# A dynamic convolution with a maxout block: one load, two warming products and one exponential moved or left out in the opening

## The chip, the cores and the metric

The kernel runs on one core of one Trainium2 chip, as one program. The metric is the device time of an execution in microseconds. Three executions of the kernel before took 410.79 to 412.25 us, with a median of 411.01 us.

## The reference

Inputs are x (8 sequences of 4160 positions with 192 features), weight_gen (for each position 8 heads with 7 logits) and three matrices: w1 and w2 (192 x 1024) and w_out (1024 x 192). Cut to what is computed:

```python
w = exp(weight_gen - max(weight_gen, -1)); w = w / (sum(w, -1) + 1e-09)
x_pad = concatenate([zeros(B, 6, D), x], axis=1)
out[b, s, h, :] = sum_k w[b, s, h, k] * x_pad[b, s + k, head h]     # 24 features to a head
h1 = out @ w1; h2 = out @ w2
result = maximum(h1, h2) @ w_out                                    # 33280 x 192, float32
```

So each position mixes itself and the six positions before it, with a softmax over the seven taps that differs by position and head, and the mixed rows go through two matrices, a maximum and a third matrix.

## The kernel before

The 33280 rows are laid over 128 partitions of 260 consecutive positions each. A "column" is one position on every partition. Columns are taken in batches of 16 (`BATCHES`); in the first two batches a batch is cut into four units of four columns, later into units of eight. The columns are rotated: what the code calls column 0 is column 8 of x (`actual`), so `load_x(0, 4, 4)`, four columns of batch 0 from its fifth on, loads columns 12 to 15 of x. The tile of x for a batch, `xb_t`, has six columns of halo and then sixteen.

The maximum is rewritten: maximum(h1, h2) @ w_out = h1 @ w_out + relu(h2 - h1) @ w_out. So the kernel forms the difference of w2 and w1 once on VectorE (`w_diff`, into `wd`, from the staged tiles `ws0` and `ws1`, whose parts are named E for the first 128 rows and T for the last 64), and the product of w1 and w_out once on TensorE (`w10_product`).

Work on a batch goes through these steps, and the lines are those that the profile names:

- `load_wg` (L115) loads logits, `load_x` (L133) loads x and converts it to bf16. `exp_sum` (L162, ScalarE) makes the exponentials, `red` (L180, VectorE) sums them over the taps, `ln` (L186, ScalarE) takes the logarithm of the sums, `shift` (L191, VectorE) subtracts it from the logits, and `weights` (L202, ScalarE) makes the softmax weights by a second exponential.
- `mul` (L218) and `mul_pair` (L227), both VectorE, multiply x by the weights for all seven taps into `m_t`. `mul_pair` takes one pair of columns, or some of its taps.
- For the early units TensorE sums the taps and transposes at once: `sum_transpose` and `sum_part` (L307) are products with the identity into `yps`, and ScalarE copies the result to `yt` (L316). Later units are summed on VectorE (`adds`, L244, L250, L253) and transposed by DMA (L262).
- `hid_tile` (L362, TensorE) multiplies `yt` by `wd`, `relu` (L372, ScalarE) moves the result to `rd_t`, and `out_first` and `out_second` (L402, L415, TensorE) form the results, which `evac` (L487, ScalarE) copies to `o_t`. In each group, `hidden` orders these steps; `relay` is an empty step on ScalarE that waits for the last product of `out_first`.

The order of the instructions on each engine is written out by hand in the opening (up to group 8, about 60 us) and follows from a table of due times later. Every engine takes its instructions in the order in which the program emits them. Loads of x go out on POOL's queue; the loads of the opening's logits and weights go out on SP's. `behind(first, load)` makes a load wait on its queue until the instruction `first` is done.

The opening matters here. SP issues the first logits, the first ten columns of x as float32 (`xs`, in three loads, converted on VectorE at L679), the first halves of the weights, the second half of the first logits, the other halves of the weights, and the second logits. VectorE's order is: sum and shift of the first half of the logits; the conversions; `mul_pair(0, 0, 0)`, the first pair's product; `mul_pair(0, 0, 1)`; `w_diff("E", 0, 0)`; `mul_pair(0, 4, 0, 0, 4)`, four taps of the second unit's first pair; `w_diff("T", 0, 2)`; `mul_pair(0, 4, 0, 4, K)`, the other three taps; `mul_pair(0, 4, 1)`; `red(0, 1, 2)`; `w_diff("E", HF, 1)`. The four taps read only columns that `xs` brought; the other three taps and the next pair read columns 12 to 15 of x. TensorE meanwhile runs products that serve no result, on a tile called `warm` (`keep_warm`, L672): 18 at the start, 8 behind the first pair's product, and 2 between the second half of `sum_transpose(0)` and `halves_swapped(2)` (L692). The latter is a product that swaps the partition halves of `wd`, copied by ScalarE at L694.

In the loop over the later groups, group 5 is the one the third edit touches. There `hidden` emits the first relu, the relay, then whatever is handed in as `amid`, the last hidden tile, the last relu, the second part of the results with their copy, and then `between`.

Of the kernel before, what the change touches and what calls it, by code (L numbers as in the profile page):

```python
# [17 lines left out]
def _sub(base: bass.AP, off: int, dims):  # L18
    ap = [list(base.ap[0])] + [[int(s), int(c)] for s, c in dims]
    return dataclasses.replace(base, offset=base.offset + off, ap=ap)  # L20
# [3 lines left out]
def kernel(  # L24
# [30 lines left out]
    def pieces(b):  # L55
        n = BATCHES[b][1]
        at, done = [], 0
        for w in (4, 4, 4, 4) if b < 2 else (8, 8) if n == 16 else (n,):
            at.append((done, w))
            done += w  # L60
        return at
# [44 lines left out]
    def actual(v):  # L106
        return v + 8 if v < LAST - 8 else v - (LAST - 8) if v < LAST else v
# [14 lines left out]
    def x_at(b, o):  # L122

        c = BATCHES[b][0] + o
        key, at = (b, o) if c < LAST - 8 else ("wrap", 0) if c < LAST else (NB - 2, 8)
        if key not in xb_ts:
            xb_ts[key] = pxb.tile([P, (16 + PAD) * D], BF16, name="xb_t", tag="xb")
        return xb_ts[key], at * D

    def load_x(b, o, n, halo=True):  # L130

        t, at = x_at(b, o)
        load = nc.gpsimd.dma_start(  # L133
            out=t[:, at + PAD * D:at + (PAD + n) * D],
            in_=bass.AP(tensor=x.tensor, offset=actual(BATCHES[b][0] + o) * D,
                        ap=[[CPP * D, P], [1, n * D]]),
        )
        if 0 < b < NB - 1 and o == 0 and halo:
            load_halo(b)
        if "wrap" in xb_ts and t is xb_ts["wrap"]:  # L140
            nc.gpsimd.memset(t[0:1, 0:PAD * D], 0.0)
            nc.gpsimd.dma_start(
                out=t[1:P, 0:PAD * D],
                in_=bass.AP(tensor=x.tensor, offset=(CPP - PAD) * D, ap=[[CPP * D, P - 1], [1, PAD * D]]),
            )
        return load
# [5 lines left out]
    def load_halo(b):  # L152

        nc.gpsimd.dma_start(out=x_at(b, 0)[0][:, 0:PAD * D],
                            in_=xb_ts[b - 1][:, 16 * D:(16 + PAD) * D])


    def exp_sum(b, i=0, of=1):
        if i == 0:
            e_ts[b] = pe_.tile([P, BATCHES[b][1] * WGC], FP32, name="e_t", tag="e")  # L160
        w = BATCHES[b][1] * WGC // of
        return nc.scalar.activation(out=e_ts[b][:, i * w:(i + 1) * w], in_=wg_ts[b][:, i * w:(i + 1) * w], func=AF.Exp)  # L162

    def part(b, i, of):

        n = BATCHES[b][1]
        h0, h1 = n * i // of * H, n * (i + 1) // of * H
        return slice(h0, h1), h0 * K, [[K, h1 - h0], [1, K]]
# [4 lines left out]
    def sums(b, hs):  # L173

        at = BATCHES[b][0] * H - (0 if b < FIRST else s_parts[0].shape[-1])
        return s_parts[b >= FIRST][:, at + hs.start:at + hs.stop]

    def red(b, i=0, of=1):
        hs, at, ap = part(b, i, of)
        nc.vector.reduce_sum(out=sums(b, hs), in_=_sub(e_ts[b], at, ap), axis=AX.X)  # L180
# [13 lines left out]
    def weights(b, o):  # L194

        w = dict(pieces(b))[o]
        if b not in en_ts:
            en_ts[b] = pen.tile([P, 16 * WGC * 2], BF16, name="en_t", tag="en")
        J = 2 if w == 4 and b < 2 else 1
        N = w * H // J  # L200
        for j in range(J):
            nc.scalar.activation(  # L202
                out=_sub(en_ts[b], (o * WGC + j * N * K) * 2, [[2 * N, K], [2, N], [1, 2]]),
                in_=_sub(wg_ts[b], (o * H + j * N) * K, [[1, K], [K, N], [0, 2]]), func=AF.Exp,
            )
# [77 lines left out]
    LEFT = (0, 1, 2, K - 1)  # L283

    def sum_transpose(u, taps=range(K), amid=lambda: None, now=True):

        copy = sum_part(u, 0, 3, taps)
        amid()
        sum_part(u, 3, 6, taps)
        if now:  # L290
            copy()
        return copy
# [32 lines left out]
    def behind(first, load):  # L325

        tc.add_manual_dep(load.ins, first.ins.name, SYNC, reason="its place among the transfers")
# [288 lines left out]
    with tc.tile_pool(name="pstage", bufs=1) as pstage:  # L616
# [40 lines left out]
        nc.vector.tensor_single_scalar(out=msk_i, in_=msk_i, scalar=RPB - 1, op=ALU.bitwise_and)  # L657
        nc.vector.tensor_single_scalar(out=msk_i, in_=msk_i, scalar=1, op=ALU.min)
        nc.vector.tensor_copy(out=msk, in_=msk_i)
        first_exp = exp_sum(0, 0, 2)  # L660
        for step in (red, ln, shift):
            step(0, 0, 2)
        weights(0, 0)
# [3 lines left out]
        def keep_warm(times, first=False):  # L667

            for _ in range(times):
                nc.tensor.matmul(warm[:, 0:512], lhsT=ident[:, 0:P],  # L672
                                 rhs=_sub(m_t, 0, [[P, 8], [1, 64]]) if first else _sub(ident, 0, [[0, 4], [1, P]]),
                                 start=True, stop=True, skip_group_check=True)

        keep_warm(18)
        for j, parts in enumerate((((0, PAD), (PAD, 2)), ((PAD + 2, 2),))):
            for at, n in parts:
                nc.vector.tensor_copy(out=xb_ts[0][:, at * D:(at + n) * D], in_=xs[:, at * D:(at + n) * D])  # L679
            first_mul = mul_pair(0, 0, j)  # L680
            if j == 0:
                keep_warm(8, True)
        w1 = {kind: pstage.tile([P, w], BF16, name="w1" + kind)
              for kind, w in (("E", F), ("T", HF))}

        def w_diff(kind, c, to):
            nc.vector.tensor_tensor(out=wd[:, to * HF:(to + 1) * HF], in0=ws[kind, 1][:, c:c + HF],
                                    in1=ws[kind, 0][:, c:c + HF], op=ALU.subtract)
# [9 lines left out]
        w1t = pstage.tile([P, F + HF], BF16, name="w1t")  # L698

        w_diff("E", 0, 0)  # L700
        behind(first_exp, load_x(0, 4, 4))
        behind(first_mul, load_x(0, 8, 4))
        load_x(0, 12, 4)
        for h in range(2):
# [8 lines left out]
            nc.sync.dma_start_transpose(out=w1t[:, c0:c0 + w].rearrange("p (b t) -> p b t", t=P), in_=w1[kind])  # L713
        mul_pair(0, 4, 0, 0, 4)
        sum_transpose(0, amid=lambda: halves_swapped(0, warm[:, 512:1024]))
        keep_warm(2)
        w_diff("T", 0, 2)
        halves_swapped(2, warm[:, 0:512])
        mul_pair(0, 4, 0, 4, K)
# [175 lines left out]
    none = lambda: None  # L895
    begun = {}

    def first_of_sum(u):
        begun[u] = sum_part(u, 0, 3)

    def rest_of_sum(u):
        sum_part(u, 3, 6)
        begun[u]()
# [2 lines left out]
        3: (none, rest_of_1),  # L906
        4: (lambda: (behind(relu_of[8], load_x(2, 0, 8, halo=False)),
                     rest_of_sum(4), behind(yt_of[4], load_wg(4, nc.gpsimd)), ln(2)), end_of_1),
        5: (lambda: (exp_sum(3), red(3), sum_transpose(5, LEFT), weights(2, 0)), none),
        6: (lambda: (weights(2, 8), ln(3), rest_of_sum(6)), none),  # L910
        7: (lambda: (behind(relu_of[14], load_x(2, 8, 8)), rest_of_sum(7)), none),
    }
# [76 lines left out]
    for g in range(4, len(GROUPS)):  # L989
        if GROUPS[g][1] == 3 and "c" not in ps:  # L990
            later_ps()
        tiles = [t for t in range(GROUPS[g][0], sum(GROUPS[g])) if t >= 16]
        if g == 9:
            behind(relu_of[16], load_x(3, 0, 8))
        if g in early:
            hidden(g, OUTS[g], early[g][0],
                   amid=lambda: first_of_sum(g) if g != 5 else None)
            early[g][1]()
            steps(g, tiles)
        else:  # L1000
            hidden(g, OUTS[g], beside=lambda: steps(g, tiles))
# [35 lines left out]
```

## Time and profile before

| | |
|---|---|
| median of three executions | 411.01 us (410.79 to 412.25) |
| the profiled execution | 411.17 us |
| its span, first to last instruction | 409.4 us |
| mean granted TensorE clock | 0.997 |
| TensorE busy | 398.0 us |
| VectorE busy | 377.2 us |
| ScalarE busy | 353.8 us |
| data moved by DMA | 66.32 MB, mean 162 GB/s |

A row of a timeline gives the start and the length in us, the engine, the line, the operation, what is written from what, and a count; in brackets the idle time of the engine just before and what ended it. PE is TensorE, PEld its weight loads, DVE VectorE, ACT ScalarE, POOL GpSimd, and SPq or POOLq are the queues' issuing. A row of the chain gives start, length and work of one piece of the chain that ended last; "issue" is time in which the engine waited for nothing that the profile shows. A row of waits gives who waited for whom, with total us, times and the longest. A row of DMA issues gives the median us from issue to landing. Consecutive instructions of an engine overlap a little, so a next one may start somewhat ahead of the end of the one before.

### The profile page before, as it was taken

The numbers are of one execution on the slowest core, as the hardware profiler recorded it, in microseconds if no ns is written. First come the engines' busy times: TensorE is split into PE (matmuls) and PEld (weight loads), VectorE is DVE, ScalarE is ACT, GpSimd is POOL, SyncE is SP. The second block draws the span as 40 slices with busy tenths as digits, with TensorE's granted clock in tenths as the row PEclk, the third lists the DMA queues.
The fourth block names the chain that finished last, engine by engine and source line by source line (L and its number), as shares of the span: only waits on it lengthen the run. The fifth ranks groups of instructions, "written<-read, shape, count | busy, mean of one in ns | idle before, by whom it ended". The sixth has DMA issues, their size and how long they took to land.

```text
span 409.4 us, 16186 instructions
## 1 busy us (share of the span) xinstructions
PE 398.0 (97%) x7406; PEld 317.0 (77%) x7406; DVE 377.2 (92%) x230; ACT 353.8 (86%) x418; POOL 81.2 (20%) x108
## 2 busy tenths in 40 slices
PE   8799999999999999999999999999999999999995
PEld 3588899777777877777777777877787777777795
DVE  6999999999999999999999999999999999999400
ACT  3889899999899998898988999999999889898781
POOL 1411012212221202221221122222111223120000
PEclk9999999999999999999999999999999999999998
DMA  8997298876657665776765676587478558835323
GB/s 242 250 176 208 66 194 152 170 170 164 162 114 210 188 141 117 231 200 87 230 186 109 143 217 188 107 214 187 103 120 250 145 107 228 171 79 158 98 79 120
DMA packets 65110, 66.32 MB, mean 162 GB/s; under 512 B 49425, under 2 KB 54161, under 8 KB 65040
## 3 DMA queue, kind: packets, MB, share of 16 engines
q1 hardware_dynamic: 56064, 40.54, 36.9%
q0 software_dynamic: 8832, 24.63, 29.3%
q8 instruction: 58, 0.95, 0.9%
q10 hardware_dynamic: 144, 0.10, 0.1%
q14 instruction: 12, 0.10, 0.1%
HBM read 37.33 MB, written 25.56 MB: 154 GB/s over the span
## 4 chain that ended last, share of the span: by engine, by line
PE 89%; ACT 6%; DMA 1%; issue 1%; SPq 1%; DVE 0%; ACTq 0%
PE op_ps L402 40%; PE hd L362 38%; PE op_ps L415 7%; ACT rd_t L372 3%; PE hdp L362 2%; PE yps L307 2%; DMA ws1T<-in_moe_w_dram 1%; ACT yt L316 1%; ACT e_t L162 0%; ACT o_t L487 0%; SPq L642 0%; ACT en_t L202 0%; SPq L625 0%; ACT xb_t L150 0%; SPq L634 0%
## 5 line engine op out<-in xcount | busy, mean ns | idle before, releaser
L372 ACT ACTIVATE rd_t<-hd 128x1024 bf16<-128x1024 f32 (+1 forms) x206 | 234.5, 1187 | 26.2 <-PE hd L362 25.0
L402 PE MATMUL op_ps<-wo,rd_t 64*128 64x192 bf16 x4160 | 210.6, 243 | 0.4 <-issue 0.4
L402 PEld LDWEIGHTS <-rd_t 64*128 64x128 bf16 x4160 | 180.8, 94 | 16.0 <-issue 0.6
L362 PE MATMUL hd<-yt,wd 64*128 64x512 bf16 (+1 forms) x1584 | 187.3, 360 | 0.4 <-ACT rd_t L372 0.4
L218 DVE TENSOR_TENSOR m_t<-xb_t,en_t 128x10752 bf16<-128x10752 bf16 (+1 forms) x35 | 181.5, 5191 | 0.8 <-ACT en_t L202 0.5
L362 PEld LDWEIGHTS <-wd 64*128 64x128 bf16 x1776 | 93.9, 94 | 44.8 <-issue 3.6
L270 POOL CAST gate<-yt 128x1 f32<-128x1 bf16 x29 | 42.1, 1451 | 257.8 <-DMA yt<-y_t 257.8
L244 DVE TENSOR_TENSOR m_t<-m_t 128x4608 bf16<-128x4608 bf16 (+1 forms) x30 | 74.1, 2470 | 0.1
L487 ACT COPY o_t<-op_ps 128x384 f32<-128x384 f32 (+1 forms) x99 | 57.1, 587 | 12.4 <-PE op_ps L402 12.4
L415 PE MATMUL op_ps<-w,yt 64*128 64x192 bf16 x768 | 54.7, 243 | 0.1
L415 PEld LDWEIGHTS <-yt 64*128 64x128 bf16 x768 | 37.8, 94 | 16.3 <-issue 1.1
L250 DVE TENSOR_TENSOR m_t<-m_t 128x3072 bf16<-128x3072 bf16 (+1 forms) x29 | 50.0, 1723 | 0.1
L202 ACT ACTIVATE en_t<-wg_t 128x896 bf16<-128x896 f32 (+2 forms) x45 | 35.8, 819 | 0.7 <-DVE wg_t L191 0.7
L253 DVE TENSOR_TENSOR y_t<-m_t 128x1536 bf16<-128x1536 bf16 (+1 forms) x29 | 27.3, 941 | 0.5
L133 POOL DMA_DIRECT2D xb_t<-in_x_dram x34 | 18.3, 538 | 32.9 <-ACT rd_t L372 22.0
L191 DVE TENSOR_TENSOR wg_t<-wg_t,ln_t 128x280 f32<-128x280 f32 (+5 forms) x46 | 22.1, 480 | 0.4 <-ACT ln_t L186 0.3
L372 ACT ACTIVATE rd_t<-hdp 128x1024 bf16<-128x1024 f32 x16 | 16.3, 1032 | 2.8 <-PE hdp L362 2.8
L162 ACT ACTIVATE e_t<-wg_t 128x896 f32<-128x896 f32 (+2 forms) x18 | 16.2, 903 | 1.3 <-DMA wg_t<-in_weight_gen_dram 1.3
L180 DVE TENSOR_REDUCE s_rest<-e_t 128x64 f32<-128x448 f32 (+2 forms) x27 | 16.3, 602 | 0.8 <-ACT e_t L162 0.8
L362 PE MATMUL hdp<-yt,wd 64*128 64x256 bf16 x192 | 13.9, 270 | 2.1 <-ACT rd_t L372 1.5
L477 DVE COPY o_last<-op_ps 128x192 f32<-128x192 f32 x1 | 0.4, 358 | 16.5 <-ACT o_last L477 16.5
L307 PE MATMUL yps<-ident,m_t 64*128 64x64 bf16 x636 | 12.5, 190 | 1.7 <-issue 1.1
(53 smaller groups left out, 89.8 us busy)
## 6 DMA issues: line engine op xcount, KB each, us to landing
out_dram<-o_t SPq DMA_DIRECT2D x22, 768.0 KB, 5.2
xb_t<-in_x_dram POOLq DMA_DIRECT2D x30, 384.0 KB, 5.1
out_dram<-o_t SPq DMA_DIRECT2D x20, 384.0 KB, 3.2
wg_t<-in_weight_gen_dram POOLq DMA_DIRECT2D x13, 448.0 KB, 5.3
xb_t<-xb_t POOLq DMA_DIRECT2D x15, 288.0 KB, 5.6
xb_t<-in_x_dram POOLq DMA_DIRECT2D x4, 192.0 KB, 6.7
xs<-in_x_dram SPq DMA_DIRECT2D x1, 576.0 KB, 3.8
ws0E<-in_moe_w_dram SPq DMA_DIRECT2D x2, 256.0 KB, 5.8
```

The source lines that it names most:

```text
L191: nc.vector.tensor_tensor(out=w_t, in0=w_t, in1=_sub(s_ts[b], hs.start, [[1, hs.stop - hs.start], [0, K]]), op=ALU.subtract)
L202: nc.scalar.activation(out=_sub(en_ts[b], (o * WGC + j * N * K) * 2, [[2 * N, K], [2, N], [1, 2]]), in_=_sub(wg_ts[b], (o * H + j * N) * K ...
L218: return nc.vector.tensor_tensor(out=m_out, in0=x_in, in1=_sub(en_ts[b], o * WGC * 2, [[2, K * n * H], [0, G // 2], [1, 2]]), op=ALU.mult,)
L244: nc.vector.tensor_tensor(out=taps(0, 1, 3), in0=taps(0, 1, 3), in1=taps(3, 1, 3), op=ALU.add)
L250: nc.vector.tensor_tensor(out=taps(0, 2, 2), in0=taps(0, 2, 2), in1=taps(1, 5, 2), op=ALU.add)
L253: nc.vector.tensor_tensor(out=_sub(y_ts[b], o * D, [[64, 2], [P, 3 * w // 2], [1, 64]]), in0=taps(0, 1, 1), in1=taps(2, 1, 1), op=ALU.add,)
L270: nc.gpsimd.tensor_copy(out=gate, in_=yt[:, 0:1])
L362: nc.tensor.matmul(hid_out(t, f, j), lhsT=wd_at(j, s, f // 4, f % 4 * P, P), rhs=_sub(yt_ts[u][half(j), :], (s + j) % 3 * P, [[3 * P, w // ...
L372: relu_of[t0] = nc.scalar.activation(out=rd[:, k * 1024:(k + n) * 1024], in_=hd[:, at:at + n * 1024], func=AF.Relu)
L402: return nc.tensor.matmul(op_out(c), lhsT=rd[half(r), k * 1024 + at:k * 1024 + at + P], rhs=wo[half(r), f * D:(f + 1) * D], start=start, s ...
L415: nc.tensor.matmul(op_out(c + j), lhsT=yt_ts[u][half(j), (3 * i + (s + j) % 3) * P:(3 * i + (s + j) % 3 + 1) * P], rhs=w10[half(j), s * D: ...
L487: nc.scalar.copy(out=_sub(o, c % 24 * D, [[D, len(qs)], [h * D, 2], [1, D]]), in_=_sub(tile_, at + (qs[0] - p) * D, [[D, len(qs)], [512, 2 ...
```

## The change

Three edits, all in the opening:

1. The load of columns 12 to 15 of x no longer waits for the first exponential but for the first pair's product. It stays the first load on POOL's queue.
2. The two warming products behind the second half of the first sums are left out.
3. The exponential of the fourth batch (`exp_sum(3)`) is handed to group 5 as `amid` and no longer stands in its `between`. On ScalarE it so stands ahead of the group's last relu and no longer behind the copy of the group's results. The relay's wait for the results of `out_first` is now carried by the exponential, where it was carried by that relu.

```diff
@@ in the opening @@
-        first_exp = exp_sum(0, 0, 2)
+        exp_sum(0, 0, 2)
         for step in (red, ln, shift):
             step(0, 0, 2)
...
             first_mul = mul_pair(0, 0, j)
             if j == 0:
+                behind(first_mul, load_x(0, 4, 4))
                 keep_warm(8, True)
...
         w_diff("E", 0, 0)
-        behind(first_exp, load_x(0, 4, 4))
         behind(first_mul, load_x(0, 8, 4))
         load_x(0, 12, 4)
...
         mul_pair(0, 4, 0, 0, 4)
         sum_transpose(0, amid=lambda: halves_swapped(0, warm[:, 512:1024]))
-        keep_warm(2)
         w_diff("T", 0, 2)
         halves_swapped(2, warm[:, 0:512])
@@ in the table of early groups @@
-        5: (lambda: (exp_sum(3), red(3), sum_transpose(5, LEFT), weights(2, 0)), none),
+        5: (lambda: (red(3), sum_transpose(5, LEFT), weights(2, 0)), none),
@@ in the loop over the groups @@
             hidden(g, OUTS[g], early[g][0],
-                   amid=lambda: first_of_sum(g) if g != 5 else None)
+                   amid=lambda: first_of_sum(g) if g != 5 else exp_sum(3))
```

Instructions on VectorE, POOL and SP keep their order. On TensorE two weight loads and two products are gone. On ScalarE one activation has another place.

## The prediction

> **What bounds the kernel now.** I read the page first: busy shares and the shares of the chain that ended last.
>
> ```profile
> span 409.4 us, 16186 instructions
> PE 398.0 (97%) x7406; PEld 317.0 (77%) x7406; DVE 377.2 (92%) x230; ACT 353.8 (86%) x418; POOL 81.2 (20%) x108
> PE 89%; ACT 6%; DMA 1%; issue 1%; SPq 1%; DVE 0%; ACTq 0%
> ```
>
> TensorE is busy for 97% of the span and carries 89% of the chain, so the whole is near a TensorE bound. Next I asked what TensorE waited for after 46 us, and got two lines in 363 us:
>
> ```profile
> PE yps L307 <- ACT yt L316: 0.5, 1, 0.5
> PE hd L362 <- ACT rd_t L372: 0.4, 2, 0.3
> ```
>
> The first of them is the wait that ends at 46.74, below. From there on TensorE runs through, and a shift that it has at 46.74 is still there at the end. All three edits lie before that. So the question is by how much TensorE is early or late at 46.74 us, and for that the opening has to be followed on its chain, in order of time (start us, us, what):
>
> ```profile
> 5.45 6.05 DMA ws1T<-in_moe_w_dram
> 12.12 0.70 DVE wd L687
> 12.86 0.39 PE warm L692
> 13.28 0.59 ACT wd L694
> 13.92 0.73 PE hdp L362 x9
> ...
> 20.96 0.83 PE hdp L362 x12
> ```
>
> The last weight piece, ws1T, lands late (issued at 5.45), VectorE's difference waits for it until 12.12, and the first hidden product follows at 13.92. The same stretch in the timeline (start, us, engine, line):
>
> ```profile
> 4.20 0.68 POOL L133 DMA_DIRECT2D xb_t<-in_x_dram  x1 [2.79 <-ACT e_t L162]
> 6.54 1.56 DVE L227 TENSOR_TENSOR m_t<-xb_t,en_t 128x2688 bf16<-128x2688 bf16 x1
> 8.47 1.56 DVE L227 TENSOR_TENSOR m_t<-xb_t,en_t 128x2688 bf16<-128x2688 bf16 x1
> 10.34 1.06 POOL L133 DMA_DIRECT2D xb_t<-in_x_dram  x2 [5.47 <-DVE m_t L227]
> 10.55 0.95 DVE L227 TENSOR_TENSOR m_t<-xb_t,en_t 128x1536 bf16<-128x1536 bf16 x1
> 11.93 0.59 PE L672 MATMUL warm<-ident 128*128 128x512 bf16 x2
> 12.12 0.69 DVE L687 TENSOR_TENSOR wd<-ws1T,ws0T 128x512 bf16<-128x512 f32 x1 [0.62 <-DMA ws1T<-in_moe_w_dram]
> 12.73 2.22 DVE L227 TENSOR_TENSOR m_t<-xb_t,en_t 128x1152 bf16<-128x1152 bf16 x2
> 14.87 0.61 DVE L180 TENSOR_REDUCE s_first<-e_t 128x64 f32<-128x448 f32 x1
> 15.02 0.88 PE L307 MATMUL yps<-ident,m_t 64*128 64x64 bf16 x42
> 15.59 0.25 ACT L186 ACTIVATE ln_t<-s_first 128x64 f32<-128x64 f32 x1
> 16.13 1.25 PE L362 MATMUL hdp<-yt,wd 64*128 64x256 bf16 x12 [0.23 <-DVE wd L687]
> ```
>
> Here the reader sees the point that decides. The product at 12.73 (the last three taps of the second unit's first pair, then its second pair) is the first to read columns 12 to 15. Behind it in VectorE's order stand the reduction of 14.87, for which ScalarE's logarithm at 15.59 waits with all of ScalarE's queue behind it, and the weight difference for which TensorE's products at 16.13 wait. TensorE's sums at 15.02 need the product itself. Whatever delays 12.73 delays all three engines alike.
>
> **Part 1, the load moved.** Before, columns 12 to 15 are issued at 4.20, 0.30 us after the first exponential's 3.32 + 0.58 = 3.90. Afterwards they wait for the first pair's product, which ends at 6.54 + 1.56 = 8.10; the second product ended at 10.03 and released its load at 10.34, so the issue falls at 8.10 + 0.31 = 8.41. POOL has nothing else between, its issue takes at most 0.68 us and is over before 10.34, so the two loads queued behind keep their time. SP's queue is not passed; its loads only have less company. When does it land? Answers on single issues (size, us from issue to landing), first the moved load as it was, then the load of 10.34, then a weight piece of SP:
>
> ```profile
> xb_t<-in_x_dram POOLq DMA_DIRECT2D x1, 192.0 KB, 6.8
> xb_t<-in_x_dram POOLq DMA_DIRECT2D x1, 192.0 KB, 6.7
> ws1T<-in_moe_w_dram SPq DMA_DIRECT2D x2, 128.0 KB, 6.6
> ```
>
> and over all 34 loads of x; below it three stretches (length, then busy us of PE, PEld, DVE, ACT and POOL; clock, DMA share, GB/s):
>
> ```profile
> DMA to landing us min/median/max: 3.8/5.2/7.5
> 15.00:17.00 2.00, 1.73 (x56) 1.20 (x54) 1.90 (x5) 2.00 (x4) 0.55 (x1) 1.00 1.18 206
> 15.00:20.00 5.00, 3.54 (x117) 2.69 (x115) 4.90 (x7) 5.00 (x10) 1.09 (x2) 1.00 1.34 204
> 15.00:40.00 25.00, 22.02 (x692) 19.91 (x690) 24.84 (x16) 22.38 (x40) 4.33 (x8) 1.00 0.97 198
> ```
>
> The DMA engines are still full after 15 us (share 1.18), and both near rows come from a full queue. The bounds are the slowest of the two near rows, 8.41 + 6.8 = 15.2, and the quickest load of x anywhere, 8.41 + 3.8 = 12.2. I take the near row less one relief: the moved load no longer stands ahead of the backlog itself. At the 206 GB/s of 15 to 17 us, when hardly anything but such converting loads ran, its 192 KB (0.197 MB) take 0.95 us. So 8.41 + 6.7 - 0.95 = 14.2.
>
> The same 0.95 us should bring ws1T from about 12.05 to 11.1. Then the difference starts when the product of 10.55 ends, at 11.50, instead of 12.12: 0.62 us sooner, and TensorE's first hidden products up to 0.5 us sooner (ScalarE's copy of the first sums, 12.02 + 0.80, holds it back a little). That gain is swallowed: VectorE then stands from 12.2 until columns 12 to 15 land. It resumes at 14.2 + 0.07 = 14.27 (0.07 as from landing 12.05 to start 12.12), where it resumed at 12.73: **+1.5 us** (bounds 12.27 - 12.73 = -0.5 and 15.27 - 12.73 = +2.5). TensorE waits for the sums of 15.02, ScalarE for the reduction, TensorE again for the second difference, each later by the same 1.5. VectorE is busy for 24.84 of the 25 us from 15 to 40, so it can't make it good, and ScalarE for all of 15 to 20, from where the chain passes to TensorE at 20.96. What was late before (ws1T) is replaced by x.
>
> **Part 2, two warming products left out.** They cost 0.59 us at 11.93, while TensorE waits for the difference until 12.86 anyway; with the difference at 12.2 they would have cost some 0.3, but TensorE then has over 1.5 us to spare before 16.5. I take 0. What they may guard is the third rival.
>
> **Part 3, the fourth exponential.** It moves on ScalarE from behind the result copy (39.80) to ahead of the relu (38.52). The rows:
>
> ```profile
> 37.34 0.49 PE L402 MATMUL op_ps<-wo,rd_t 64*128 64x192 bf16 x7 [0.42 <-issue]
> 38.52 1.02 ACT L372 ACTIVATE rd_t<-hdp 128x1024 bf16<-128x1024 f32 x1 [0.92 <-PE hdp L362]
> 39.80 0.96 ACT L162 ACTIVATE e_t<-wg_t 128x896 f32<-128x896 f32 x1
> 40.65 0.80 ACT L316 CAST yt<-yps 128x768 bf16<-128x768 f32 x1
> 40.52 0.88 PE L402 MATMUL op_ps<-wo,rd_t 64*128 64x192 bf16 x16
> 41.50 0.33 PE L307 MATMUL yps<-ident,m_t 64*128 64x64 bf16 x11
> 46.74 0.79 PE L307 MATMUL yps<-ident,m_t 64*128 64x64 bf16 x42 [0.46 <-ACT yt L316]
> ```
>
> ScalarE idles 0.92 us ahead of the relu. The exponential now inherits the wait for the group's first results (the wait that stood ahead of the relu), which end at 37.34 + 0.49 = 37.83. So it runs from 37.87, frees ScalarE after 0.85 (39.80 to 40.65) at 38.72, and the relu starts 0.2 late; its readers come a group later. The result copy ends 0.2 later, at 40.1, just ahead of its next use by TensorE. The copy of the sums moves from 40.65 to about 40.0. TensorE's next sums wait for that copy, until 41.50; their engine is free at 40.52 + 16 x 0.041 = 41.18 (the chain charges 0.66 us for 16 of these). Gain 0.3 us; what is late next is TensorE itself. The relu after follows TensorE and ScalarE's chain then runs to the wait at 46.74, so 0.3 arrives there. The weights of the fourth batch were issued 8 us earlier and are there. Bounds: 0, if the relu or the result copy holds TensorE, and -0.3, for TensorE is busy before 41.18. I take -0.3.
>
> **Sum.** The profiled execution took 411.17 us (span 409.4, and 1.8 around it); the median of the runs shown is 411.01, 0.16 less. 411.17 + 1.5 + 0 - 0.3 = 412.4; against the median **412.2 us**, 0.3% slower. About 0.5% (2.1 us) is what I count as telling a change of this kernel from none.
>
> **Rivals.** First, the load is hidden: it lands by 12.2, as quick as the quickest load of x. VectorE resumes at 12.27 where it did at 12.73, and with the exponential the sum is -0.5 - 0.3: 410.2, faster than before. It decides at a landing of about 13.0 (4.6 us after issue), where delay and gain cancel. For it speaks the median of 5.2 and SP's shrinking backlog (its last issue was at 8.99); against it both rows from a full queue, 6.7 and 6.8. The mechanism behind would be turns between the two queues: then SP's backlog does not stand ahead of POOL's load. The Trainium skill, "DMA: Bandwidth & Descriptors", section "Queues, rings and completion order", says that each DMA engine takes turns between the queues that have work for it, a packet at a time; by that rule this rival would be right, and the trace agrees badly, since 192 KB took 6.7 us beside SP's loads.
>
> Second, no relief: the load takes the full 6.8 us and the exponential gives nothing. VectorE resumes at 15.27, +2.5 and 0: 413.5 against the median, 0.6% slower. For it speaks that SP's loads may simply close the gap.
>
> Third, TensorE's clock. The opening shows that TensorE is slow after rest, though the granted clock reads 1.00:
>
> ```profile
> 1.64 6.85 PE L672 MATMUL warm<-ident 128*128 128x512 bf16 x18 [1.64 <-DVE ident L655]
> 8.33 1.89 PE L672 MATMUL warm<-m_t,ident 128*128 128x512 bf16 x8
> ```
>
> 18 products in 6.85 us (0.38 each), later 8 in 1.89 (0.24 each). Afterwards TensorE has some 0.2 us of work between 11.9 and 13.4, and rests from about 14.8 until 16.6. If that makes it slow again, the work that now lies in 15 to 20 us (3.54 us busy of 5) doubles, and the 1.46 us of idle time there take some of it: +2.1 on top, 414.3. Against it: no rest is longer than 2 us. The Trainium skill, "TensorE: Matmul & The Clock Gate", section "HAM oscillation — how this bites in real kernels", warns of idle gaps over about 3.4 us; by that rule the clock holds here, but the two products left out were work in this very stretch, and no run here shows where the limit lies.
>
> **Chances.** Forecast (landing between 13.3 and 15.0, so 411.3 to 413.0): 0.65. Hidden load, 410.2 to 411.3: 0.15. No relief, 413.1 to 413.8: 0.12. Slow clock, 414 and over: 0.08. Faster by over 0.5% would be under 409.0, which no case reaches; I leave 0.03. Slower by over 0.5% is over 413.1: 0.12 + 0.08 and a little of the forecast's upper end, 0.22. Within: 0.75. The range takes in the hidden load and the missing relief: 410.2 to 413.8.
>
> **What would show it.** Right: issue of columns 12 to 15 at 8.4; VectorE idle over 1 us until 14.3, released by that load and no longer by ws1T; first hidden products at about 13.4; sums of 15.02 and logarithm of 15.59 later by 1.5; the fourth exponential inside ScalarE's idle time before the relu; no wait of TensorE for the copy at 41.5; from 46.7 on the same shift to the end. Wrong: VectorE idle ends before 13, or the products of 15 to 20 us are longer each.

## The result and the profile after

The changed kernel takes 412.79 us in the median of 7 executions (411.97 to 414.51) against 410.79 us for the kernel before, also 7. The ratio is 1.0054, with a 95% interval from 1.0032 to 1.0075: some 2.0 to 2.2 us slower, about the 0.5% that was to count as telling; the interval lies on both sides of it. The forecast was 412.2 us in a range of 410.2 to 413.8, with a chance of 0.22 for slower by over 0.5%. Ratios are of fast executions alone, and one execution of the load behind the shift (418.16 us, in its median below) counts as slow.

The profiled execution of the changed kernel took 413.78 us, with a span of 412.0. First the page, then the chain in order of time (start us, us, what):

```profile
span 412.0 us, 16182 instructions
...
PE 398.3 (97%) x7404; PEld 317.3 (77%) x7404; DVE 377.4 (92%) x230; ACT 354.0 (86%) x418; POOL 79.9 (19%) x108
...
PE 89%; ACT 5%; DMA 2%; DVE 2%; issue 1%; ACTq 0%
```

```profile
6.59 1.56 DVE m_t L227
...
8.46 5.82 DMA xb_t<-in_x_dram
14.28 0.02 issue
...
17.71 0.28 PE hdp L362 x2
...
23.26 0.83 PE hdp L362 x12
...
404.81 1.99 PE op_ps L402 x48
```

The last row of before's chain that stands against the last one here:

```profile
402.73 1.99 PE op_ps L402 x48
```

The busy times of TensorE, VectorE and ScalarE are those of before within half a microsecond; TensorE is simply later. The chain no longer runs through ws1T but through the moved load, issued at 8.46 and landed at 14.28. The row that was at 20.96 before is at 23.26, 2.3 us later, TensorE's sums that were at 46.74 start at 48.81, and the last group of results starts at 404.81, both 2.1 us later. The timeline shows what happens in between (start, us, engine, line; in brackets the idle time before):

```profile
8.46 0.68 POOL L133 DMA_DIRECT2D xb_t<-in_x_dram  x1 [7.05 <-DVE xb_t L679]
...
11.47 0.69 DVE L688 TENSOR_TENSOR wd<-ws1T,ws0T 128x512 bf16<-128x512 f32 x1
...
12.86 1.86 PE L362 MATMUL hdp<-yt,wd 64*128 64x256 bf16 x24 [0.26 <-ACT yt L316]
...
14.30 2.23 DVE L227 TENSOR_TENSOR m_t<-xb_t,en_t 128x1152 bf16<-128x1152 bf16 x2 [2.14 <-DMA xb_t<-in_x_dram]
...
16.58 0.79 PE L307 MATMUL yps<-ident,m_t 64*128 64x64 bf16 x42 [1.86 <-DVE m_t L227]
...
17.09 0.26 ACT L186 ACTIVATE ln_t<-s_first 128x64 f32<-128x64 f32 x1 [1.96 <-DVE s_first L180]
...
17.71 1.51 PE L362 MATMUL hdp<-yt,wd 64*128 64x256 bf16 x12 [0.34 <-DVE wd L688]
...
18.81 1.37 PE L307 MATMUL yps<-ident,m_t 64*128 64x64 bf16 x39
...
20.14 1.47 PE L362 MATMUL hdp<-yt,wd 64*128 64x256 bf16 x11
```

The row of 8.46 names the conversion of L679, which ended just before, as releaser. The issue comes 0.31 us after the end of the first pair's product (8.15), the same lag as that of 0.30 and 0.31 us behind the instructions that released the loads of before.

The weight difference of ws1T no longer waits (11.47 instead of 12.12). VectorE instead idles 2.14 us for columns 12 to 15, and TensorE (1.86 us) and ScalarE (1.96 us) idle behind it. Then there is a second thing: the 39 sums of 18.81 take 1.37 us, where before 39 of them took 0.79, and the hidden products of 17.71 and 20.14 are stretched likewise. The rows of before:

```profile
17.12 0.79 PE L307 MATMUL yps<-ident,m_t 64*128 64x64 bf16 x39
...
17.84 0.81 PE L362 MATMUL hdp<-yt,wd 64*128 64x256 bf16 x11
```

### The profile page after: what moved, and what is told of

Same layout as the page of the kernel before. It is cut to its first block, busy times and chain, and to the rows that moved or that the text cites. A ratio compares the mean times of both kernels' runs of the same rounds, so it can differ in the third digit from the quotient of the medians.

```text
span 412.0 us, 16182 instructions
## 1 busy us (share of the span) xinstructions
PE 398.3 (97%) x7404; PEld 317.3 (77%) x7404; DVE 377.4 (92%) x230; ACT 354.0 (86%) x418; POOL 79.9 (19%) x108
## 4 chain that ended last, share of the span: by engine, by line
PE 89%; ACT 5%; DMA 2%; DVE 2%; issue 1%; ACTq 0%
PE op_ps L402 40%; PE hd L362 38%; PE op_ps L415 7%; ACT rd_t L372 3%; PE yps L307 2%; PE hdp L362 2%; DMA xb_t<-in_x_dram 1%; DVE m_t L227 1%; DMA wg_t<-in_weight_gen_dram 1%; ACT en_t L202 0%; ACT o_t L487 0%; ACT yt L316 0%; ACT xb_t L150 0%; DVE s_first L180 0%; ACT e_t L162 0%
## 5 line engine op out<-in xcount | busy, mean ns | idle before, releaser
L270 POOL CAST gate<-yt 128x1 f32<-128x1 bf16 x29 | 40.8, 1406 | 259.5 <-DMA yt<-y_t 259.5
L362 PE MATMUL hdp<-yt,wd 64*128 64x256 bf16 x192 | 14.9, 280 | 1.6 <-ACT rd_t L372 0.8
```

Of the source, the lines that this page charges most:

```text
L270: nc.gpsimd.tensor_copy(out=gate, in_=yt[:, 0:1])
L362: nc.tensor.matmul(hid_out(t, f, j), lhsT=wd_at(j, s, f // 4, f % 4 * P, P), rhs=_sub(yt_ts[u][half(j), :], (s + j) % 3 * P, [[3 * P, w // ...
```

## The experiments

The kernels, with the time, its ratio to runs of the kernel before on the same chip (their medians are 410.63 to 411.19 us, so the times of two rows can't be compared directly), and three marks from one profiled execution each: when VectorE starts the product that needs columns 12 to 15, when TensorE starts the hidden products that were at 20.96, and when the last group of results starts (us).

| kernel | median us | ratio (95% interval) | product | hidden | last group |
|---|---|---|---|---|---|
| before | 410.79 | 1 | 12.73 | 20.96 | 402.73 |
| before, second profile | 412.50 (one) | | 12.50 | 20.74 | 403.33 |
| changed | 412.79 | 1.0054 (1.0032 to 1.0075) | 14.30 | 23.26 | 404.81 |
| changed, second profile | 415.63 (one) | | 15.03 | 24.16 | 406.40 |
| load alone | 413.16 | 1.0056 (1.0037 to 1.0076) | 14.28 | 22.48 | 404.06 |
| without the load | 410.47 | 0.9994 (0.9979 to 1.0009) | 12.14 | 20.46 | 401.88 |
| changed, rest filled | 412.91 | 1.0056 (1.0036 to 1.0076) | 14.55 | 22.75 | 403.98 |
| load behind the shift | 411.02 | 1.0003 (0.9989 to 1.0016) | 12.02 | 20.44 | 403.00 |
| exponential alone | 411.25 | 1.0000 (0.9986 to 1.0014) | 12.71 | 20.94 | 402.81 |
| load behind the weights | 411.94 | 1.0019 (1.0001 to 1.0036) | 13.92 | 22.62 | 403.50 |
| logits later | 412.58 | 1.0051 (1.0032 to 1.0071) | 12.11 | 20.74 | 403.29 |
| combined | 411.09 | 1.0015 (1.0002 to 1.0028) | 12.10 | 20.48 | 405.73 |

### The load alone, and all but the load

The first of these two kernels makes the first edit only, the second only the other two.

```diff
 # the load alone (against before)
+                behind(first_mul, load_x(0, 4, 4))
-        behind(first_exp, load_x(0, 4, 4))
```

> The kernel before with the moved load alone; the two warming products and the place of the fourth exponential stay as before. Theory A (the load's landing sets the loss): VectorE waits for columns 12 to 15 until 14.3, as in the changed kernel (14.30, where before has 12.73), TensorE's sums follow at 16.6, and the whole is 1.5 to 2.2 us slower than before. Theory B (TensorE's clock falls because the two warming products are gone): the sums still start at 16.6, but the hidden products of 16 to 22 us take about 270 ns each as before and not the 355 ns of the changed kernel, and the loss is 0.7 us smaller than in the changed kernel. If the rest alone does it, they take 355 ns here too. Theory C (the exponential's new place costs something): this one is faster than the changed kernel by 0.3 us or more.

```diff
 # without the load (against before)
-        keep_warm(2)
-        5: (lambda: (exp_sum(3), red(3), sum_transpose(5, LEFT), weights(2, 0)), none),
+        5: (lambda: (red(3), sum_transpose(5, LEFT), weights(2, 0)), none),
-                   amid=lambda: first_of_sum(g) if g != 5 else None)
+                   amid=lambda: first_of_sum(g) if g != 5 else exp_sum(3))
```

> The changed kernel with its load put back behind the first exponential: only the two warming products are gone and the fourth exponential stands ahead of the relu. Theory A: VectorE's product starts at 12.73 again and the time is that of before within 0.4 us. By the recorded sum it would be 0.3 us faster. By the reading that the sums after 41.5 us are held by TensorE's own instruction stream next (a stall that ends at 42.16 in before), the exponential gains nothing: 0.0, and the wait at 42.16 stays there while that at 41.50 goes. Theory B (the two products guard the clock): hidden products of 13 to 18 us over 300 ns each, and 0.5 us or more slower than before.

Measured: 1.0056 with the load alone, 0.9994 without it. The load carries the loss, and the other two edits together are worth nothing that can be measured (between 0.9 us of gain and 0.4 us of loss). Theory A holds, and nothing speaks for C. With the load alone the wait is the same as in the changed kernel, and here TensorE's products keep their pace after the rest:

```profile
14.28 2.23 DVE L227 TENSOR_TENSOR m_t<-xb_t,en_t 128x1152 bf16<-128x1152 bf16 x2 [2.13 <-DMA xb_t<-in_x_dram]
...
16.57 0.79 PE L307 MATMUL yps<-ident,m_t 64*128 64x64 bf16 x42 [1.79 <-DVE m_t L227]
...
18.68 0.79 PE L307 MATMUL yps<-ident,m_t 64*128 64x64 bf16 x39
```

That looks like theory B, that the two products guard the clock; but its second half, 0.7 us less loss, did not come: 1.0056 is no less than 1.0054 (the two intervals together leave some 1.2 us either way).

### The rest filled, and the load issued in between

In the changed kernel eight products are put where TensorE rests; in two other kernels the load waits for something else.

```diff
 # the rest filled (against the changed kernel)
-        features = sum_part(1, 0, 3)
+        features = sum_part(1, 0, 3, fill=8)
 # and in sum_part
+        for _ in range(fill):
+            nc.tensor.matmul(yps[:, 0:512], lhsT=ident[:, 0:P], rhs=_sub(ident, 0, [[0, 4], [1, P]]),
+                             start=True, stop=True, skip_group_check=True)
```

> The changed kernel with eight products of 512 columns put on TensorE ahead of the second unit's sums, where it otherwise rests from 14.3 to 16.6; they write to the bank that the sums then overwrite, so nothing of the result changes. Clock theory: the products after the rest take 270 ns (hidden) and 190 ns (sums) again where the changed kernel has 355 and 214 for 16 to 22 us, and the copy at 20.38 comes 0.5 to 0.7 us sooner. What arrives at the end is 0 to 0.7 us, since stalls in TensorE's instruction stream between 30 and 45 us may take the gain. Rival (the products are slow for another reason, the load of the memory by the DMA or the order of operands): they stay at 355 ns, and the copy at 20.38 stays.

Measured: TensorE's pace is back, but nothing of it shows in the median (1.0056). The granted clock of TensorE in the changed kernel, in stretches before, in and after the slow products (length; busy us of PE, PEld, DVE, ACT, POOL; clock, DMA share, GB/s):

```profile
14.00:17.00 3.00, 1.14 (x41) 0.81 (x39) 2.70 (x4) 1.02 (x1) 0.55 (x1) 1.00 1.16 205
18.00:19.00 1.00, 0.96 (x14) 0.61 (x15) 0.96 (x3) 1.00 (x2) 0.28 (x1) 0.86 1.60 198
19.00:22.00 3.00, 2.62 (x57) 1.89 (x52) 3.00 (x3) 2.39 (x6) 0.00 (x0) 0.50 1.20 250
22.00:23.00 1.00, 0.83 (x12) 0.64 (x12) 1.00 (x2) 1.00 (x3) 0.00 (x0) 0.94 1.81 171
```

The clock goes to half from some 18.7 to 22.1 us. The groups of TensorE by form there (16 to 22 us):

```profile
L362 PE MATMUL hdp<-yt,wd 64*128 64x256 bf16 x24 | 3.1, 355 | 0.4 <-DVE wd L688 0.3
L307 PE MATMUL yps<-ident,m_t 64*128 64x64 bf16 x84 | 2.3, 214 | 1.9 <-DVE m_t L227 1.9
```

and the timeline of the kernel with the rest filled:

```profile
14.64 1.90 PE L304 MATMUL yps<-ident 128*128 128x512 bf16 x8
...
16.83 0.79 PE L310 MATMUL yps<-ident,m_t 64*128 64x64 bf16 x42 [0.29 <-DVE m_t L227]
...
18.95 0.79 PE L310 MATMUL yps<-ident,m_t 64*128 64x64 bf16 x39
```

There the clock reads 1.00 throughout this stretch. So the slow stretch is the halved clock. One profile can't show that it comes from the rest, since the load alone rested 1.79 us and kept its pace too. The mean granted clock of whole executions, which is on record for 161 of them, shows more: it is 0.995 or lower in 12 of the 30 executions of the three kernels with such a rest that is not filled (the changed kernel 5 of 8, the load alone 4 of 10, the load behind the weights, below, 3 of 12), in none of the 7 with the rest filled, and in one of the 124 others. So the rest brings the slow clock in a part of the executions, and with the rest filled it was not seen. The rival (memory traffic, operands) falls, for nothing else was changed.

```diff
 # load behind the shift, with the second and third edit (against before; shift now returns its instruction)
-        first_exp = exp_sum(0, 0, 2)
+        exp_sum(0, 0, 2)
-            step(0, 0, 2)
+            first_shift = step(0, 0, 2)
-        behind(first_exp, load_x(0, 4, 4))
+        behind(first_shift, load_x(0, 4, 4))
 # load behind the weights, nothing else (against before; weights now returns its last instruction)
-        weights(0, 4)
+        first_weights = weights(0, 4)
-        behind(first_exp, load_x(0, 4, 4))
+        behind(first_weights, load_x(0, 4, 4))
```

> The changed kernel with the load of columns 12 to 15 waiting for the first shift on VectorE (done at 5.50), so issued at about 5.8, between 4.2 (before) and 8.46 (after). With 5.8 us from issue to landing, as the moved load has in the changed kernel, it lands at 11.6; with 6.8, at 12.6. Theory A says that VectorE's product of 12.73 starts when the later of this load and the weight difference is there: at 12.2 to 12.7, and the time is 0 to 0.6 us below before. If instead ws1T is the one held up by any load issued ahead of 8 us, VectorE waits for ws1T until 12.1 again and the time is that of before within 0.3 us.

> The kernel before with the load of columns 12 to 15 waiting for the last of the first weights on ScalarE (done at 6.87), so issued at about 7.2, and nothing else changed. Theory A (the landing sets the loss): with 5.8 us to landing it lands at 13.0, VectorE waits for it and resumes at 13.05, 1.2 us ahead of the changed kernel, and the time lies between the two: 0.3 to 0.9 us over before and at least 1 us under the kernel with the load alone moved. Rival (any load behind the weights' pieces pays the whole price, or none): the time of before, or 413.

Measured: issued at 5.80, the load is there in time (product at 12.02, no wait) and the time is that of before. TensorE's hidden products start at 20.44 there, 0.5 us sooner than at 20.96, but TensorE later stops for 1.49 us where before stopped for 0.33 (below, What TensorE stops for). Issued at 7.33, the load lands 6.6 us later and not 5.8 as expected, VectorE waits 1.38 us and resumes at 13.92, not at 13.05; the time is 1.0019, between the two kernels. It lies 0.8 us above before, as foretold, where the load alone lies 2.3 us above it. So the price is not the delay itself: a product that is 1.5 us later than the average one of before (12.44, below) cost 0.8 us here. The row of that wait, and TensorE's after it:

```profile
13.92 2.23 DVE L228 TENSOR_TENSOR m_t<-xb_t,en_t 128x1152 bf16<-128x1152 bf16 x2 [1.38 <-DMA xb_t<-in_x_dram]
...
16.20 0.79 PE L308 MATMUL yps<-ident,m_t 64*128 64x64 bf16 x42 [1.18 <-DVE m_t L228]
...
18.31 1.23 PE L308 MATMUL yps<-ident,m_t 64*128 64x64 bf16 x39
```

This kernel keeps the two warming products and rests only 1.18 us, and yet the 39 sums take 1.23 us. So theory B falls too: the two products don't keep the clock up. Four profiles have this rest ahead of the sums and do not fill it (1.18 to 2.53 us): the changed kernel twice, the load behind the weights, and the load alone. In three the clock fell to 0.50, 0.7 to 2.3 us after the rest ended, each time for 3.41 us; in the load alone and in the other eight profiles it fell only after the last product. The length of the rest alone does not decide. Before has one of 1.19 us as well, a little later, and its clock stayed at 1.00:

```profile
19.84 0.83 PE L362 MATMUL hdp<-yt,wd 64*128 64x256 bf16 x12 [1.19 <-ACT rd_t L372]
```

All nine profiles whose clock stayed up have such a rest, of 1.16 to 1.20 us, at 18 to 20.5 us. What the traces add is a grid: every stretch of one clock that they record from its start to its end lasts a whole multiple of 3.41 us (13.65 or 4 times, and 389.12 or 114 times, in the changed kernel; 399.36 or 117 times in before), and where the grid lies differs by execution. In the three that fell the clock first reached full speed at 4.4 to 5.1 us, in the load alone at 6.87, in the kernel with the rest filled at 4.46. That the place of the rest on this grid decides would fit, and is not shown.

### The exponential alone

```diff
 # against before: only the third edit
-        5: (lambda: (exp_sum(3), red(3), sum_transpose(5, LEFT), weights(2, 0)), none),
+        5: (lambda: (red(3), sum_transpose(5, LEFT), weights(2, 0)), none),
-                   amid=lambda: first_of_sum(g) if g != 5 else None)
+                   amid=lambda: first_of_sum(g) if g != 5 else exp_sum(3))
```

> The kernel before with the fourth exponential ahead of the relu and nothing else. By the recorded sum: 0.3 us faster than before. By the reading that TensorE's instruction stream is next (a stall at the 1728th instruction, ended at 42.16 in before): the wait of TensorE for the copy of the sums at 41.5 goes, the stall at that instruction ends at the same distance from the stall at the 1472nd (4.8 us), and the time is that of before within 0.2 us. Rival (the relu held back by the exponential costs something): slower by 0.2 us or more, with a wait of TensorE for the relu or for the result copy between 39 and 42 us.

Measured: 1.0000 (0.9986 to 1.0014). The interval, some 0.6 us either way, takes in the 0.3 us that were expected, so the time does not decide here; the rows do. This execution agrees with that of before to a few hundredths of a microsecond from 12 to 38 us, so they can be laid side by side:

```profile
37.34 0.49 PE L402 MATMUL op_ps<-wo,rd_t 64*128 64x192 bf16 x7 [0.42 <-issue]
...
38.02 0.95 ACT L162 ACTIVATE e_t<-wg_t 128x896 f32<-128x896 f32 x1 [0.42 <-PE op_ps L402]
...
38.88 1.01 ACT L372 ACTIVATE rd_t<-hdp 128x1024 bf16<-128x1024 f32 x1
...
40.14 0.81 ACT L316 CAST yt<-yps 128x768 bf16<-128x768 f32 x1
...
41.21 0.34 PE L307 MATMUL yps<-ident,m_t 64*128 64x64 bf16 x11
...
42.17 0.62 PE L307 MATMUL yps<-ident,m_t 64*128 64x64 bf16 x31 [0.61 <-issue]
```

The exponential does run in the idle time, the copy of the sums comes 0.51 us sooner (40.14, not 40.65), and TensorE's sums start at 41.21, not 41.50: the 0.3 us are won. Eleven sums later TensorE stops for 0.61 us, where before it stopped for 0.33, and goes on at 42.17, where before it was 42.16. The gain is given back within a microsecond, and the sums of 46.74 start at 46.74 again.

### What TensorE stops for

These stops have no releaser in the profile. Counted in TensorE's own order, weight loads and products together, they stand at the same positions wherever they occur: before instruction 960, 1216, 1472 and 1728 (and 704 with the load alone), which are 256 apart. In before, 466 products and as many loads stand ahead of the sums of 28.51, 932 instructions; 14 loads and 13 products of these sums run, and the stop stands before the 960th instruction. The changed kernel has four instructions less ahead of these places, and the last two stops stand two products later in the program, after 11 and 13 products of their group where before they stood after 9 and 11; with eight products more, they stand after 3 and 5. In us from the chain of before, of the changed kernel and of the one with the rest filled:

```profile
28.82 0.52 issue
...
32.76 0.30 issue
...
36.92 0.42 issue
...
41.83 0.33 issue
```

```profile
38.53 0.91 issue
...
43.60 0.67 issue
```

```profile
37.44 0.67 issue
...
42.51 0.69 issue
```

A row of the page's queues gives the size: packets, MB, share.

```profile
q8 instruction: 58, 0.95, 0.9%
```

0.95 MB in 58 packets is 16.4 KB each, and TensorE's 7406 products and 7406 weight loads, in blocks of 256, are 58 blocks. So TensorE seems to wait there for the next block of its own instructions. The times of these packets in the traces settle it (us from the span's start):

| profile | stop before instruction | packet starts | packet lands | TensorE goes on | after the landing |
|---|---|---|---|---|---|
| before | 960 | 26.94 | 27.84 | 29.33 | 1.49 |
| before | 1216 | 30.78 | 31.66 | 33.06 | 1.40 |
| before | 1472 | 35.01 | 35.94 | 37.34 | 1.40 |
| before | 1728 | 39.80 | 40.82 | 42.16 | 1.34 |
| exponential alone | 1728 | 39.91 | 40.92 | 42.17 | 1.25 |
| combined | 1216 | 33.03 | 33.91 | 35.53 | 1.62 |

In the twelve profiles there are 38 stops of TensorE of over 0.11 us without a releaser. All stand at these places, and all end 1.25 to 1.62 us after a packet of this queue landed. At none of the 672 such places, 56 in each profile, does TensorE go on sooner than 1.22 us after the landing of the packet that belongs to it by the count, stop or no stop. So TensorE waits for the block. With the exponential alone the block lands 0.10 us later than in before, though TensorE is 0.3 us sooner at the place: the end of the stop hangs on the block. What makes a block late is open. Two runs asked whether other loads hold the blocks back:

```diff
 # logits later (against before): the fifth batch's logits behind a later load of x
-                     rest_of_sum(4), behind(yt_of[4], load_wg(4, nc.gpsimd)), ln(2)), end_of_1),
+                     rest_of_sum(4), ln(2)), end_of_1),
-        7: (lambda: (behind(relu_of[14], load_x(2, 8, 8)), rest_of_sum(7)), none),
+        7: (lambda: (behind(relu_of[14], load_x(2, 8, 8)), load_wg(4, nc.gpsimd), rest_of_sum(7)), none),
 # combined: this, the load behind the shift, and the third edit
```

> The kernel before with one later load moved: the logits of the fifth batch, issued at 36.77, now follow the load of x at 47.90. Question: what ends the stalls of TensorE that have no releaser and stand at its instructions 960, 1216, 1472 and 1728. If the loads of data hold back the stream of instructions, the stalls at the 1472nd and 1728th (0.42 and 0.33 us in before, 0.42 and 0.61 with the exponential moved) get shorter, the DMA share of 36 to 42 us falls from 0.81, and the time falls by up to 0.7 us. If the stream comes at its own pace, they stay within 0.2 us and so does the time.

> The kernel before with three edits: the load of columns 12 to 15 behind the first shift (issued at 5.8), the logits of the fifth batch later as in the other run, and the fourth exponential ahead of the relu; the two warming products stay. If the stream of instructions can be relieved by moving the logits, the 0.5 to 0.7 us that the earlier product wins by 21 us and the 0.3 us of the exponential arrive at the end: 0.5 to 1.2 us under before. If not, the gain is eaten by the stalls at the 1472nd and 1728th instruction, as with the load behind the shift before (1.49 us at the 1728th), and the time is that of before within 0.4 us.

Measured: with the logits later, the DMA share of 36 to 42 us fell from 0.81 to 0.60, but the stop at the 1472nd instruction is 0.42 us again and that at the 960th 1.00. There is none at the 1728th, but the second profile of before, below, has none there either. The time is 1.0051, slower. Why is open; its profiled execution, at 411.07 us, was its fastest. Both kernels with the logits later have stops past 50 us, which none of the other ten profiles has: 0.54 us until 56.37 here, 0.17 and 0.18 us until 58.56 and 64.76 in the combined one. The moved load may have shifted the lateness there; that is not shown. Combined, the 0.5 us won at 20.48 did not arrive (1.0015), and its profiled execution, 414.77 us and its slowest, had these stops:

```profile
28.34 1.55 issue
...
33.31 2.22 issue
...
39.39 0.97 issue
```

Added up, the stops come to 1.57 and 2.39 us in the two profiles of before, to 1.58 and 2.31 in those of the changed kernel, and to 0.59 to 5.09 in all twelve. So within one kernel they differ by more than the 0.3 or 0.5 us that two of the edits won ahead of them, and moving that load does not shorten them. No version tried is measurably faster than the kernel before.

### A second profile of both kernels

> The kernel before once more, for another profile of it. In the kernel with the load left in place and the other two edits made, VectorE did not wait for ws1T and resumed at 12.14, where the first profile of before shows 12.73 after a wait of 0.62. If that wait belongs to the kernel, it is here again. If it belongs to that one execution, the weight difference starts at about 11.5 here and the product at 12.1; then the moved load costs VectorE 2.1 us against the usual execution of before and not 1.6, which is what the medians differ by.

> The changed kernel once more. The load lands within 0.4 us of 14.3, the hidden products after TensorE's rest take about 355 ns again if the rest and the missing products make TensorE slow each time, and about 270 if it hung on the moment; the stalls without a releaser stand at the 1472nd and 1728th instruction again, with other lengths.

Measured: in the second profile of before the weight difference waits 0.26 us and the product starts at 12.50. Its row names no releaser, but the last piece of ws1T, issued at about 5.4, took 6.4 us and so landed at the end of this wait. In the changed kernel the load lands later still:

```profile
15.03 2.23 DVE L227 TENSOR_TENSOR m_t<-xb_t,en_t 128x1152 bf16<-128x1152 bf16 x2 [2.81 <-DMA xb_t<-in_x_dram]
...
17.31 0.79 PE L307 MATMUL yps<-ident,m_t 64*128 64x64 bf16 x42 [2.53 <-DVE m_t L227]
```

The wait for ws1T neither belongs to the kernel nor to one execution: it lies between 0 and 0.62 us. Five profiles with the load in its old place (before twice, the exponential alone, without the load, logits later) give 12.73, 12.50, 12.71, 12.14 and 12.11 for the product, on average 12.44. Four with the load behind the first pair's product give 14.30, 15.03, 14.28 and 14.55, on average 14.54. The difference is 2.1 us.

## Why the prediction was right, and where it was not

**The moved load.** Right in mechanism, too small in size. It said issue at 8.41, landing at 14.2 and VectorE back at 14.27; the first profile showed 8.46, 14.28 and 14.30. That the gain on ws1T would be swallowed and that all three engines would be late alike was right: 1.57 us at the product, 1.56 at TensorE's sums, 1.50 at ScalarE's logarithm. That ws1T would come 0.95 us sooner was nearly right: from issue to landing (median of its two pieces) it took 6.0 to 6.6 us in the five profiles with the load in its old place, 6.4 on average, and 5.2 to 5.9 in the four with the load at about 8.4, 5.5 on average. What was mis-sized is the term of 1.5 us, by 0.3 at both its ends: the product starts at 14.54 on average and not at 14.27, and the 12.73 of the one profiled execution of before is the late end of a range (12.1 to 12.7, 12.44 on average). Against the usual execution the delay is 2.1 us, not 1.5. The estimate of 5.75 us to landing stands against 5.8, 5.8, 6.1 and 6.5 for the loads issued at about 8.4.

**The rival of the hidden load** did not come about. The load would have had to land by 13.0. By the rule of the Trainium skill, "DMA: Bandwidth & Descriptors", section "Queues, rings and completion order", that the DMA engines take turns between queues, it should have come sooner; no load of these columns issued from 7.3 us on took under 5.8 us beside SP's queue.

**The two warming products.** The 0 us agrees: without them, with the exponential moved and the load in its old place, nothing is lost that can be measured.

**The fourth exponential.** This is the step that failed. Its working was right as far as the copy, down to the 0.3 us by which TensorE's sums start sooner. Its last sentence was wrong: "what is late next is TensorE itself". Next is the stop at TensorE's 1728th instruction, which stood in the very chain that was read, 0.33 us behind the row quoted, marked "issue". It ends when the block of instructions is there, at 42.16 and 42.17, whether TensorE reaches it 0.3 us sooner or not. The term is 0.0 in that profile, not -0.3; by the median alone it lies within 0.6 us of nothing.

**The slow clock**, given 0.08, did come about in the profile, with a rest of under 2 us: the clock stood at 0.50 for about 3.4 us, the hidden products of 16 to 22 us took 355 ns each instead of about 270, and the row of 20.96 came 2.30 us late and not 1.57. The prediction would have had +2 us; it was 0.7 by 23 us, for only 3.4 us were slow. Whether the 0.7 us reach the end is open. By the medians nothing does, filled or not, but their intervals leave some 1.2 us either way; in the single profiles the changed kernel is 0.78 us behind the load alone at the hidden products and still 0.75 at the last group. The stops don't take it up: those of before at 28.82 and 32.76, 0.82 us together, are gone in the changed kernel, but its other two are 0.83 us longer. The prediction read a granted clock of 1.00 in the opening. That was no reading: in the trace of before the first record of the clock stands at 7.33 us, and TensorE's first products start 0.43 us apart until then and 0.22 us apart from then on. The rule of the Trainium skill, "TensorE: Matmul & The Clock Gate", section "HAM oscillation — how this bites in real kernels", warns of gaps over about 3.4 us. The half clock and the length of 3.4 us agree with the Trainium skill; the length of the gap does not, since the clock fell after rests of 1.18, 1.86 and 2.53 us, and the measurement decides.

**The sum.** 1.5 - 0.3 = 1.2 us was forecast and 2.0 to 2.2 measured. With the delay as the profiles show it and the exponential at nothing, it is 2.1 + 0.0 = 2.1. Both errors go the same way, so nothing cancelled; the range had room for them. The forecast of 412.2 stands 0.6 us under the 412.79, and not 0.8 as the differences do, since the median of before is 410.79 with seven executions and not 411.01. The agreement of 2.1 with the measured time is within its interval and no proof that a delay arrives in full: the load behind the weights was 1.5 us late at the product and cost 0.8.

## What to carry to other kernels

A load that is moved behind a later event is priced by its time to land in the queue as it then is, and by the earliest moment at which its reader could otherwise start; take that moment from several profiles, because a wait that stands in one profile may be absent in the next. Before a gain on the chain is booked, read the chain a microsecond further: a stop marked "issue" that stands at a fixed place in an engine's instructions ended here when the block of instructions was there, and took back what was won just ahead of it.

## What the runs showed of the hardware

TensorE stopped for its own instructions at places 256 of them apart, for up to 2.2 us a stop, and went on 1.25 to 1.62 us after a packet of 16.4 KB of the instruction queue had landed. That was in a stretch where it takes 256 instructions in about 3.4 us (from the end of the stop at 28.82, 29.33, to the next stop at 32.76). From 50 us on, where the chain has longer products, only three such stops are left in the twelve profiles. From the hidden products of the table to the last group of results it takes 380.9 to 382.6 us in eleven profiles and 385.3 in the combined one, so a delay or a gain ahead of the stops arrives changed by up to some 1.7 us, in most.

A rest of TensorE of 1.2 to 2.5 us ahead of the sums was followed, 0.7 to 2.3 us after its end, by 3.41 us at half the granted clock, in three profiles of four and by the mean clock in 12 executions of 30. Rests of 1.16 to 1.20 us at 18 to 20.5 us, in the nine other profiles, were not.
